# Joined pair operands, single-piece loads, VectorE copies and three product lumps in the backward pass of a fused attention and SwiGLU block

## The chip, the cores and the metric

The kernel runs on one core of a Trainium2 chip. The metric is the device time of one execution in microseconds (us), lower being better. Engines are named as in the profile: PE is TensorE, DVE is VectorE, ACT is ScalarE, POOL is GpSimd, SP is SyncE, which only issues DMAs here.

## The reference

The program computes a forward value and all gradients of a residual block in which attention and a SwiGLU feed-forward layer stand side by side on one layer norm. Sizes: 2048 tokens, model width 448, 16 heads of 28, feed-forward width 1792, bf16 inputs.

```python
xn  = layernorm(x)                                   # no scale, no bias
q, k, v = split_heads(xn @ wqkv)                     # 16 heads, Dh = 28
o   = softmax(q @ k.T * Dh**-0.5) @ v
out = x + merge_heads(o) @ wo + (silu(xn @ w_gate) * (xn @ w_up)) @ w_down
# outputs: out, and the gradients of <out, grad_out> for x, wqkv, wo, w_gate, w_up, w_down
```

## The kernel before, in words

The order of the instructions on each engine is written out by hand; nothing reorders them. The work has three stages.

**Stage one** (0 to about 642 us) is the layer norm, the projections, the attention forward and the feed-forward forward and backward. PE works through score products with feed-forward and weight-gradient products as fillers. At the end of the projections of a group of four heads (`proj_done`) POOL stores the transposed q, k and v of the group to DRAM tensors `qT_d`, `kT_d` and `vT_d`; at the end of each query block (`o_items`, its inner `do`) it stores the transposed, scaled output gradient to `dOT_d`. The attention's `load_pair` reads these back later.

**Stage two** (about 642 to 1465 us) is the attention backward. There are 8 pairs of heads (`pr`), two to a group (`g`). For each pair, four key chunks `kc` of 512 keys, and for each of them two windows of 8 query tiles: 512 *units* `k`, 64 *windows* `W`. The unit's place in its window is `pos`, 0 to 7. For a unit PE computes the scores of two heads into a PSUM tile (`sd`, line 851), and one unit later the gradients of the probabilities into another (`sd`, line 862). ACT takes the exponential (`E`, line 869). DVE multiplies the two into `ds` (line 880). Three units later `acc_mm` (line 748) adds the unit's share to the gradients of k and v. The pool `ps_sd` has three buffers: the scores of unit k need that `ds` of unit k-3 is done, and the second product of unit k needs that the exponential of unit k is done.

The gradient of q needs `ds` transposed, into a tile `dsT` per window. Six of the 8 units of a window are transposed by a DMA that SP issues right after `ds` is written (line 882). The two units in `TQ` are transposed on PE instead (`pe_transpose`, line 775, eight 128x128 transposes into the single PSUM buffer `aux`) and copied to `dsT` by `tr_out` (line 782): unit 1 of the window at the end of `pos` 6, by DVE, and unit 4 at `pos` 0 of the next window, by ACT. The pool of `ds` has 8 buffers: DVE can write `ds` of a unit only when the transposing DMA of the unit 8 earlier has landed. `dq_mm` (line 795) multiplies a window's `dsT` at `pos` 5 two windows later, and `dq_out` adds the result up on DVE at `pos` 6.

Each window also carries a *job* on PE from the list `jobs`, into the same `aux` buffer: a token tile of the block's output (`y`, 19 products of 448 columns, windows 1 to 16), a tile of one of two partial gradients of x (`dx`, 14 products), a chunk of the gradient of wqkv (`dwq`), or nothing. The products are issued in four lumps, at `pos` 1 to 4; ACT copies the result out at `pos` 4.

SP issues in one order: the job's tile for window W+2 at `pos` 0 (`job_load`, lines 660 to 666), the six transposes of a window, the transposes of finished gradients, and at `pos` 4 pieces of three lists: `pload`, the next pair's operands (`load_pair`, line 552); `gload`, the next group's (`load_group`, line 563); `wload`, the next weight matrix (line 539). A pair's operands are two tiles, `qT` and `kT`. Each has 64 partitions from one DRAM tensor and 64 from another, loaded in two column pieces: 8 DMAs of 128 KB. Up to two pieces of `pload`, one of `gload` and two of `wload` go out per window.

**The tail** (about 1465 us to the end) finishes the last chunks of the gradient of wqkv and, for each of 16 token tiles, adds up the gradient of x on PE and takes it back through the layer norm: `g_sb` on ACT, `junk`, `bb`, `cc` on DVE, `t1` on ACT (line 974), `t2` on DVE (976), the sum `dx` on POOL (979), the store by SP (980).

Of the kernel before, what the change touches and what calls it, by code (L numbers as in the profile page):

```python
# [10 lines left out]
ALU = mybir.AluOpType  # L11
AX = mybir.AxisListType
FP32 = mybir.dt.float32
BF16 = mybir.dt.bfloat16
# [3 lines left out]
S = 2048  # L18
D = 448
# [3 lines left out]
G = 4  # L23
HP = 32
P = 128
NT = S // P
# [11 lines left out]
def kernel(  # L38
# [19 lines left out]
    pe, act, dve, pool, sp = nc.tensor, nc.scalar, nc.vector, nc.gpsimd, nc.sync  # L58
# [4 lines left out]
    out1_d = out_1.rearrange("b (t p) d -> p (b t) d", p=P)  # L63

    dram = ctx.enter_context(tc.tile_pool(name="dram", bufs=1, space=DRAM))
    qT_d = dram.tile([G, P, S], BF16, name="qT_d")
    kT_d = dram.tile([G, P, S], BF16, name="kT_d")
    vT_d = dram.tile([G, P, S], BF16, name="vT_d")
    dOT_d = dram.tile([G, P, S], BF16, name="dOT_d")
    spq_d = dram.tile([G, P, NT * P], BF16, name="spq_d")  # L70
    spk_d = dram.tile([G, P, NT * P], BF16, name="spk_d")
    spo_d = dram.tile([G, P, NT * P], BF16, name="spo_d")
# [15 lines left out]
    xn_sp = const.tile([P, NT, DP], BF16, name="xn_sp")  # L88
# [109 lines left out]
    def proj_done(g):  # L198

        qT, kT, vT = (qk_tiles[(g, i)] for i in range(3))  # L200
        if g > 0:
            v = v_tiles[g] = qkp.tile([P, NT, P], BF16, name="v_sp")
            sp.dma_start_transpose(out=v[:], in_=vT[:])
        pool.dma_start(out=vT_d[g], in_=vT[:])
        pool.dma_start(out=qT_d[g], in_=qT[:])
        pool.dma_start(out=kT_d[g], in_=kT[:])

    def sp_layout(g, tq):
        s_ = stg.tile([P, NT, P], BF16, name="sp_stage")
# [256 lines left out]
    def o_items(g, qc, o_ps):  # L466
# [4 lines left out]
        st = {}  # L471
# [24 lines left out]
        def do(i):  # L496
            if i == 0:
                st["do"] = ps_f.tile([P, 4, P], FP32, name="f_ps")
            for c in range(4):
                pe.matmul(st["do"][:, i, :], lhsT=dyT[:, 4 * qc + i, c, :], rhs=woT[:, c, g * P:(g + 1) * P],  # L500
                          start=(c == 0), stop=(c == 3))
            if i < 3:
                return
            dps = st["do"][:].rearrange("p t (h r) -> p (t h) r", r=HP)
            rlb = st["rlc"][:].rearrange("p t h -> p (t h)")
            prod = op_.tile([P, 16, HP], FP32, name="prod")
            dve.tensor_tensor(out=prod[:], in0=dps,
                              in1=O_sp[g][:, tsl, :].rearrange("p t (h r) -> p (t h) r", r=HP), op=ALU.mult)
            delta = op_.tile([P, 16], FP32, name="delta")
            dve.tensor_reduce(out=delta[:], in_=prod[:, :, 0:DH], axis=AX.X, op=ALU.add)  # L510
            dOl = op_.tile([P, 4, P], BF16, name="dOl")
            dOv = dOl[:].rearrange("p t (h r) -> p (t h) r", r=HP)
            dve.tensor_tensor(out=dOv, in0=dps, in1=rlb.unsqueeze(2).to_broadcast([P, 16, HP]), op=ALU.mult)
            ndl = op_.tile([P, 16], FP32, name="ndl")
            dve.scalar_tensor_tensor(out=ndl[:], in0=delta[:], scalar=-1.0, in1=rlb, op0=ALU.mult, op1=ALU.mult)
            dve.tensor_copy(out=dOv[:, :, 28], in_=ndl[:])
            lo = op_.tile([P, 16], FP32, name="lo")
            dve.tensor_tensor(out=lo[:], in0=ndl[:], in1=dOv[:, :, 28], op=ALU.subtract)
            dve.tensor_copy(out=dOv[:, :, 29], in_=lo[:])
            pool.dma_start(out=spo_d[g, :, 4 * qc * P:(4 * qc + 4) * P], in_=dOl[:].rearrange("p t c -> p (t c)"))  # L520
            dT = op_.tile([P, 512], BF16, name="dOT")
            sp.dma_start_transpose(out=dT[:].rearrange("p (t s) -> p t s", t=4),
                                   in_=dOl[:].rearrange("p t c -> p (t c)"))
            pool.dma_start(out=dOT_d[g, :, qc * 512:(qc + 1) * 512], in_=dT[:])

        push([[(0.2, lambda i=i: tr(i)) for i in range(4)], [(0.26, lambda i=i: do(i)) for i in range(4)]]
             + (dwo_items(g) if qc == 3 else []), front=True, behind=1)
# [16 lines left out]

    def load_pair(pr, parts):

        g, r = pr // 2, 64 * (pr % 2)
        q = qkp.tile([P, S], BF16, name="qT")
        k = qkp.tile([P, S], BF16, name="kT")
        qd[pr] = (q, k)  # L550
        n = S // parts
        return [lambda i=i, dst=dst, r0=r0, src=src: sp.dma_start(
                    out=dst[r0:r0 + 64, i:i + n], in_=src[g, r:r + 64, i:i + n])
                for r0, srcs in ((0, (qT_d, kT_d)), (64, (dOT_d, vT_d)))
                for dst, src in zip((q, k), srcs) for i in range(0, S, n)]

    def load_group(g, parts, kpool):

# [206 lines left out]
                    in_=o[r:r + 64, :].rearrange("p (k s) -> p k s", k=2))  # L765
        sp_later.append(later)

    TQ = (1, 4)

    def pe_transpose(W, qi):  # L770

# [3 lines left out]
            pe.transpose(ps[:, i, :], ds[:, i // 4, (i % 4) * P:(i % 4 + 1) * P], ident_bf[:])  # L775
        st["tr"] = (ps, dsT[:, :, :, qi * P:(qi + 1) * P])

    def tr_out(eng):

        ps, dst = st["tr"]  # L780
        out, in_ = dst.rearrange("p j c q -> p (j c) q"), ps[:]
        act.copy(out=out, in_=in_) if eng is act else dve.tensor_copy(out=out, in_=in_)  # L782

    def dq_mm(W, half):
        pr, kc, w, _ = units[W * UW]
# [44 lines left out]
    for k in range(N + 2 * UW):  # L830
        W, pos = k // UW, k % UW
        if k < N:
# [7 lines left out]
            if pos == 4:  # L840
                if W == len(jobs) - 1:
                    wload.extend(load_w("wq", 2))
                for lst, n in ((pload, 2), (gload, 1), (wload, 2)):
                    for f in lst[:n]:
                        f()
                    del lst[:n]
# [3 lines left out]
            for j in range(2):  # L850
                pe.matmul(s_ps[:, j, :], lhsT=q[HP * j:HP * j + HP, qt * P:(qt + 1) * P],  # L851
                          rhs=kv[HP * j:HP * j + HP, kc * 512:(kc + 1) * 512],
                          start=True, stop=True, tile_position=(HP * j, 0))
        late_tr = pos == 0 and 1 <= W <= NW
        if 1 <= k <= N:
            pr, kc, w, qi = units[k - 1]
            q, kv = qd[pr]
# [10 lines left out]
            E[k] = ework.tile([P, 2, 512], BF16, name="E")  # L868
            act.activation(out=E[k][:], in_=s_ps[:], func=ACT.Exp, scale=SCALE)  # L869
        if late_tr:  # L870
            tr_out(act)
        job = jobs[W] if W < len(jobs) else None
        if pos == 6 and 2 <= W <= NW + 1:
            dq_out(W - 2)
# [9 lines left out]
        while sp_later:  # L884
            sp_later.pop(0)()

        if pos == 1:
            if 3 <= k < N + 3:
                acc_mm(k - 3)
            if job:  # L890
                st["aux"] = ps_x.tile([P, 512], FP32, name="aux")
                fillers = job_mms(W, st["aux"])
        if 1 <= pos < 5 and job:
            n = -(-len(fillers) // (5 - pos))
            for f in fillers[:n]:
                f()
            fillers = fillers[n:]
        if k == N + UW + 5:
            for c in range(4):
                if c % 2 == 0:  # L900
# [5 lines left out]
        if pos == 5 and 2 <= W <= NW + 1:  # L906
            dq_mm(W - 2, 0)
            dq_mm(W - 2, 1)
        if pos != 1 and 3 <= k < N + 3:
            acc_mm(k - 3)  # L910
        if pos == 4 and job:
            job_out(W, st["aux"])
        if pos == 6 and W < NW:
            pe_transpose(W, TQ[0])
            tr_out(dve)
    while sp_later:
        sp_later.pop(0)()
    ast.close()
# [2 lines left out]
    with ExitStack() as fin:  # L921
# [20 lines left out]
        for part in range(2):  # L942
            for c, (ps, m) in enumerate(last_dwq):
                for f in m[part][12 * (1 - part):]:
                    f()
                if part == 1:
                    dwq_out(3, c, ps)
        wq = wtile["wq"]
        for t in range(NT):
            if t % 2 == 0:  # L950
                load_c(t // 2 + 3, act)
# [5 lines left out]
            for n in range(3 * G):  # L957
# [14 lines left out]
                                     op0=ALU.mult, op1=ALU.mult)  # L972
            t1 = wk.tile([P, D], FP32, name="t1")
            act.activation(out=t1[:], in_=g_ps, func=ACT.Identity, scale=rstd[:, t:t + 1], bias=bb[:, 0:1])
            t2 = wk.tile([P, D], FP32, name="t2")
            dve.scalar_tensor_tensor(out=t2[:], in0=xn_sp[:, t, :D], scalar=cc[:, 0:1], in1=t1[:],
                                     op0=ALU.mult, op1=ALU.add)
            dx = wk.tile([P, D], BF16, name="dx")
            pool.tensor_tensor(out=dx[:], in0=t2[:], in1=dy_t[:, t, :], op=ALU.add)
            sp.dma_start(out=out1_d[:, t, :], in_=dx[:])  # L980
    cst.close()


# [28 lines left out]
```

## Time and profile before

| what | us |
|---|---|
| three runs | 1529.53, 1534.82, 1534.94 |
| median of them | 1534.82 |
| the profiled execution | 1534.68 |
| its span, first to last instruction | 1532.9 |
| mean granted clock of PE in it | 0.979 |

The times of the prediction below are worked out against the profiled execution, whose time is 0.14 us under the median of the runs. In the rows, "x57" is a count, "mean ns" is the mean duration of one instruction, and the last field tells for how long the engine stood idle before these instructions and what ended that. "SPq" is SP issuing a DMA. "issue" is time in which the engine waited for nothing that the profile shows.

### The profile page before, as it was taken

Reading aid. Unit: us, or ns where it says so; the run is one execution under the profiler, and the core shown is the slowest. Engines: PE = TensorE matmul, PEld = TensorE weight load, DVE = VectorE, ACT = ScalarE, POOL = GpSimd, SP = SyncE. Lnnn points to the kernel's source line nnn. Section 1 sums busy time; section 2 is a strip of 40 time slices with the busy share of each in tenths; the row PEclk is TensorE's granted clock in tenths of the full one; section 3 lists DMA queues with packets and bytes.
Section 4 is the critical chain, followed back from the end, with each engine's and each line's share of the span. In section 5 each row is a group of like instructions: output and inputs, shape, how many; then the busy total and the mean of one; then the engine's idle time right before and its main releaser. Section 6 shows DMA issues by size and latency. Waiting matters only on the chain.

```text
span 1532.9 us, 32019 instructions
## 1 busy us (share of the span) xinstructions
PE 1414.2 (92%) x12176; PEld 600.1 (39%) x12176; DVE 1100.7 (72%) x1421; ACT 1187.9 (77%) x1333; POOL 395.0 (26%) x664
## 2 busy tenths in 40 slices
PE   6899999999999999798989988989899899999987
PEld 3233333333333333333334344334345343544353
DVE  7664555656666667377878878888788788888925
ACT  6898998889888888576767777778778778788823
POOL 4332443344435444400111121101112101111033
PEclk9999999999999999889999999999999999999999
DMA  9976767878877799799999999999999999999984
GB/s 216 190 157 144 156 122 157 171 136 169 173 166 144 159 190 214 178 197 208 218 206 207 185 194 209 197 204 206 208 195 197 198 205 183 180 190 211 186 272 140
DMA packets 682106, 285.12 MB, mean 186 GB/s; under 512 B 637136, under 2 KB 650464, under 8 KB 681952
## 3 DMA queue, kind: packets, MB, share of 16 engines
q1 hardware_dynamic: 652016, 210.03, 75.5%
q0 software_dynamic: 25968, 64.53, 17.2%
q10 hardware_dynamic: 3968, 8.52, 1.7%
q8 instruction: 95, 1.56, 0.4%
q14 instruction: 59, 0.48, 0.1%
HBM read 67.34 MB, written 63.44 MB: 85 GB/s over the span
## 4 chain that ended last, share of the span: by engine, by line
PE 59%; ACT 13%; DMA 12%; DVE 8%; issue 6%; POOL 1%; SPq 0%; DVEq 0%; ACTq 0%; POOLq 0%
DMA dsT<-ds 9%; PE f_ps L356 8%; PE s_ps L599 7%; PE f_ps L382 7%; PE sd L851 6%; ACT E L869 5%; PE aux L718 5%; PE acc L748 4%; PE o_ps L581 4%; ACT eT L604 4%; PE aux L775 4%; DVE ds L880 4%; PE aux L795 3%; ACT dsT L782 3%; PE f_ps L180 3%
## 5 line engine op out<-in xcount | busy, mean ns | idle before, releaser
L880 DVE TENSOR_TENSOR ds<-sd,E 128x1024 bf16<-128x1024 f32 x512 | 611.5, 1219 | 134.0 <-PE sd L862 49.8
L869 ACT ACTIVATE E<-sd 128x1024 bf16<-128x1024 f32 x512 | 516.7, 1023 | 175.6 <-PE sd L862 136.5
L604 ACT ACTIVATE eT<-s_ps 128x1024 bf16<-128x1024 f32 x512 | 497.2, 1025 | 79.5 <-PE s_ps L599 76.1
L862 PE MATMUL sd<-kT,qT 32*128 32x512 bf16 x1024 | 203.4, 390 | 22.2 <-ACT E L869 21.3
L851 PE MATMUL sd<-kT,qT 32*128 32x512 bf16 x1024 | 202.7, 392 | 20.6 <-DVE ds L880 18.0
L748 PE MATMUL acc<-ds,v_sp 128*32 128x512 bf16 x1024 | 205.3, 396 | 0.7 <-DVE ds L880 0.7
L748 PE MATMUL acc<-E,O_sp 128*32 128x512 bf16 x1024 | 205.1, 396 | 0.2 <-ACT dkv_o L754 0.2
L599 PE MATMUL s_ps<-qT,kT 32*128 32x512 bf16 x1024 | 152.8, 383 | 10.1 <-ACT eT L604 7.9
L421 POOL DMA_DIRECT2D hd_d<-fT x168 | 126.9, 773 | 18.5 <-DVE fT L416 5.3
L382 PE MATMUL f_ps<-xnT,wgu 128*128 128x512 bf16 x448 | 117.6, 381 | 1.7 <-DVE w_sb L408 1.5
L763 POOL DMA_DIRECT2D dqkv_d<-dkv_o x64 | 39.2, 616 | 293.3 <-ACT dkv_o L754 291.4
L718 PE MATMUL aux<-W,ck 128*128 128x448 bf16 x448 | 107.5, 357 | 3.3
L851 PEld LDWEIGHTS <-qT 32*128 32x128 bf16 x1024 | 51.2, 91 | 150.0 <-issue 141.2
L581 PE MATMUL o_ps<-eT,v_sp 128*32 128x512 bf16 x1024 | 102.8, 391 | 0.0
L356 PE MATMUL f_ps<-xn_sp,f_sp 128*128 128x448 bf16 x448 | 99.7, 356 | 0.0
L599 PEld LDWEIGHTS <-kT 32*128 32x128 bf16 x1024 | 42.4, 90 | 143.5 <-issue 136.8
L748 PEld LDWEIGHTS <-O_sp 128*32 128x32 bf16 x1024 | 50.3, 93 | 113.5 <-issue 104.0
L775 PE MATMUL aux<-ident_bf,ds 128*128 128x128 bf16 x1024 | 81.3, 224 | 13.5 <-DVE dq_acc L807 6.5
L356 PEld LDWEIGHTS <-f_sp 128*128 128x128 bf16 x672 | 58.3, 98 | 78.6 <-issue 23.5
L862 PEld LDWEIGHTS <-qT 32*128 32x128 bf16 x1024 | 65.2, 91 | 60.5 <-issue 56.5
L775 PEld LDWEIGHTS <-ds 128*128 128x128 bf16 x1024 | 63.5, 99 | 42.4 <-issue 41.7
L394 DVE SCALAR_TENSOR_TENSOR g<-t_sb,f_ps 128x512 f32<-128x512 f32 x56 | 38.4, 686 | 54.0 <-ACT t_sb L392 53.9
(133 smaller groups left out, 1763.1 us busy)
## 6 DMA issues: line engine op xcount, KB each, us to landing
hd_d<-fT POOLq DMA_DIRECT2D x168, 128.0 KB, 4.6
ck<-hd_d SPq DMA_DIRECT2D x32, 448.0 KB, 4.3
ck<-hd_d SPq DMA_DIRECT2D x16, 576.0 KB, 4.9
dsT<-ds SPq DMA_TRANSPOSE x384, 4.2
dqkv_d<-dkv_o POOLq DMA_DIRECT2D x64, 64.0 KB, 3.8
dq_c<-dqkv_d ACTq DMA_DIRECT2D x5, 768.0 KB, 6.1
W<-wT_d SPq DMA_DIRECT2D x14, 224.0 KB, 3.6
out_dram<-dw_o POOLq DMA_DIRECT2D x28, 96.0 KB, 3.7
```

Of the source, the lines that this page charges most:

```text
L356: pe.matmul(acc[:, :D], lhsT=src[:, 12 * (t // 4) + 4 * wi + t % 4, :], rhs=rhs[:, t, :D], start=(t == 0), stop=(t == NT - 1))
L382: pe.matmul(st[name][:], lhsT=w(c), rhs=src[:, tsl, c, :], start=(c == 0), stop=(c == 3))
L581: pe.matmul(o_ps[HP * hh:HP * (hh + 1), :], lhsT=v[:, kt, HP * hh:HP * (hh + 1)], rhs=e[hh // 2][:, hh % 2, :], start=(kt == 0), stop=(kt ...
L599: pe.matmul(s_ps[:, j, :], lhsT=kT[r:r + HP, kt * P:(kt + 1) * P], rhs=qT[r:r + HP, qc * 512:(qc + 1) * 512], start=True, stop=True, tile_ ...
L604: act.activation(out=e[:], in_=s_ps[:], func=ACT.Exp, scale=SCALE)
L718: return [lambda n=n: pe.matmul(ps[:, :D], lhsT=t[:, n, :], rhs=w[:, n, :], start=(n == 0), stop=(n == NFC - 1)) for n in range(NFC)]
L748: pe.matmul(acc[r:r + HP, :], lhsT=src[:, qt, 64 * hp + HP * j:64 * hp + HP * j + HP], rhs=m[:, j, :], start=(qt == 0), stop=(qt == NT - 1 ...
L775: pe.transpose(ps[:, i, :], ds[:, i // 4, (i % 4) * P:(i % 4 + 1) * P], ident_bf[:])
L851: pe.matmul(s_ps[:, j, :], lhsT=q[HP * j:HP * j + HP, qt * P:(qt + 1) * P], rhs=kv[HP * j:HP * j + HP, kc * 512:(kc + 1) * 512], start=Tru ...
L862: pe.matmul(d_ps[:, j, :], lhsT=q[r:r + HP, qt * P:(qt + 1) * P], rhs=kv[r:r + HP, kc * 512:(kc + 1) * 512], start=True, stop=True, tile_p ...
L869: act.activation(out=E[k][:], in_=s_ps[:], func=ACT.Exp, scale=SCALE)
L880: dve.tensor_tensor(out=DS[k - 1][:], in0=d_ps[:], in1=E[k - 1][:], op=ALU.mult)
```

## The change

- **DRAM layout.** Four tensors become two with one entry per pair: `qdo_d` has q on the first 64 partitions and the output gradient on the others, `kv_d` has k and v. The stores in stage one are halved accordingly: `proj_done` issues 6 instead of 3, `do` 2 instead of 1, each with 64 partitions.
- **Loads.** `load_pair` makes a DMA of 128 partitions of each tile, in two column pieces: 4 DMAs of 256 KB for a pair. One piece goes out in an even window and one piece of `gload` in an odd one.
- **Transposes on PE.** `TQ` is (2, 6). Unit 2 is transposed at the end of `pos` 6 and copied after the multiplication of `pos` 7; unit 6 is transposed at `pos` 1 of the next window and copied before the multiplication there. DVE makes both copies.
- **Products.** A job's products go in three lumps, at `pos` 2 to 4; at `pos` 2 `acc_mm` stands ahead of the lump.
- **Tail.** `t2`, the sum and the store of a token tile are issued after `t1` of the next one (`finish`), and the last three sums are on DVE instead of POOL.

```diff
-    qT_d = dram.tile([G, P, S], BF16, name="qT_d")
-    kT_d = dram.tile([G, P, S], BF16, name="kT_d")
-    vT_d = dram.tile([G, P, S], BF16, name="vT_d")
-    dOT_d = dram.tile([G, P, S], BF16, name="dOT_d")
+    qdo_d = dram.tile([2 * G, P, S], BF16, name="qdo_d")
+    kv_d = dram.tile([2 * G, P, S], BF16, name="kv_d")
...
-        pool.dma_start(out=vT_d[g], in_=vT[:])
-        pool.dma_start(out=qT_d[g], in_=qT[:])
-        pool.dma_start(out=kT_d[g], in_=kT[:])
+        for hp in range(2):
+            rows = slice(64 * hp, 64 * hp + 64)
+            for dst, src in ((kv_d[2 * g + hp, 64:], vT), (qdo_d[2 * g + hp, :64], qT), (kv_d[2 * g + hp, :64], kT)):
+                pool.dma_start(out=dst, in_=src[rows, :])
...
-            pool.dma_start(out=dOT_d[g, :, qc * 512:(qc + 1) * 512], in_=dT[:])
+            for hp in range(2):
+                pool.dma_start(out=qdo_d[2 * g + hp, 64:, qc * 512:(qc + 1) * 512],
+                               in_=dT[64 * hp:64 * hp + 64, :])
...
-        return [lambda i=i, dst=dst, r0=r0, src=src: sp.dma_start(
-                    out=dst[r0:r0 + 64, i:i + n], in_=src[g, r:r + 64, i:i + n])
-                for r0, srcs in ((0, (qT_d, kT_d)), (64, (dOT_d, vT_d)))
-                for dst, src in zip((q, k), srcs) for i in range(0, S, n)]
+        return [lambda i=i, dst=dst, src=src: sp.dma_start(out=dst[:, i:i + n], in_=src[pr, :, i:i + n])
+                for i in range(0, S, n) for dst, src in ((q, qdo_d), (k, kv_d))]
...
-    TQ = (1, 4)
+    TQ = (2, 6)
...
-    def tr_out(eng):
-
+    def tr_out():
         ps, dst = st["tr"]
-        out, in_ = dst.rearrange("p j c q -> p (j c) q"), ps[:]
-        act.copy(out=out, in_=in_) if eng is act else dve.tensor_copy(out=out, in_=in_)
+        dve.tensor_copy(out=dst.rearrange("p j c q -> p (j c) q"), in_=ps[:])
...
-                for lst, n in ((pload, 2), (gload, 1), (wload, 2)):
+                for lst, n in ((pload, 1 - W % 2), (gload, W % 2), (wload, 2)):
...
-        late_tr = pos == 0 and 1 <= W <= NW
+        late_tr = pos == 1 and 1 <= W <= NW
...
         if late_tr:
-            tr_out(act)
+            tr_out()
...
-        if pos == 1:
-            if 3 <= k < N + 3:
-                acc_mm(k - 3)
-            if job:
-                st["aux"] = ps_x.tile([P, 512], FP32, name="aux")
-                fillers = job_mms(W, st["aux"])
-        if 1 <= pos < 5 and job:
+        if pos == 7 and W < NW:
+            tr_out()
+        acc = 3 <= k < N + 3
+        if pos == 2 and job:
+            st["aux"] = ps_x.tile([P, 512], FP32, name="aux")
+            fillers = job_mms(W, st["aux"])
+        lump = []
+        if 2 <= pos < 5 and job:
             n = -(-len(fillers) // (5 - pos))
-            for f in fillers[:n]:
-                f()
-            fillers = fillers[n:]
+            lump, fillers = fillers[:n], fillers[n:]
+        if acc and pos == 2:
+            acc_mm(k - 3)
+        for f in lump:
+            f()
+        if acc and pos != 2:
+            acc_mm(k - 3)
...
-        if pos != 1 and 3 <= k < N + 3:
-            acc_mm(k - 3)
...
         if pos == 6 and W < NW:
             pe_transpose(W, TQ[0])
-            tr_out(dve)
...
+        def finish(t, t1, cc):
+            t2 = wk.tile([P, D], FP32, name="t2")
+            dve.scalar_tensor_tensor(out=t2[:], in0=xn_sp[:, t, :D], scalar=cc[:, 0:1], in1=t1[:],
+                                     op0=ALU.mult, op1=ALU.add)
+            dx = wk.tile([P, D], BF16, name="dx")
+            add = pool if t < NT - 3 else dve
+            add.tensor_tensor(out=dx[:], in0=t2[:], in1=dy_t[:, t, :], op=ALU.add)
+            sp.dma_start(out=out1_d[:, t, :], in_=dx[:])
...
-            t2 = wk.tile([P, D], FP32, name="t2")
-            dve.scalar_tensor_tensor(out=t2[:], in0=xn_sp[:, t, :D], scalar=cc[:, 0:1], in1=t1[:],
-                                     op0=ALU.mult, op1=ALU.add)
-            dx = wk.tile([P, D], BF16, name="dx")
-            pool.tensor_tensor(out=dx[:], in0=t2[:], in1=dy_t[:, t, :], op=ALU.add)
-            sp.dma_start(out=out1_d[:, t, :], in_=dx[:])
+            if t > 0:
+                finish(t - 1, *held)
+            held = (t1, cc)
+        finish(NT - 1, *held)
```

1 line of the change is left out of this document (removed).

## The prediction

> **What bounds the kernel now.** I read the page first: the shares of the engines, the chain that ended last, and the groups of instructions, with shapes kept apart.
>
> ```profile
> PE 1414.2 (92%) x12176; PEld 600.1 (39%) x12176; DVE 1100.7 (72%) x1421; ACT 1187.9 (77%) x1333; POOL 395.0 (26%) x664
> DMA dsT<-ds 9%; PE f_ps L356 8%; PE s_ps L599 7%; PE f_ps L382 7%; PE sd L851 6%; ACT E L869 5%; PE aux L718 5%; PE acc L748 4%; PE o_ps L581 4%; ACT eT L604 4%; PE aux L775 4%; DVE ds L880 4%; PE aux L795 3%; ACT dsT L782 3%; PE f_ps L180 3%
> ...
> L880 DVE TENSOR_TENSOR ds<-sd,E 128x1024 bf16<-128x1024 f32 x512 | 611.5, 1219 | 134.0 <-PE sd L862 49.8 <-DMA dsT<-ds 46.6 <-issue 14.3
> L782 ACT COPY dsT<-aux 128x1024 bf16<-128x1024 bf16 x64 | 64.8, 1012 | 8.9 <-PE aux L775 1.5 <-DMA dsT<-ds 0.6
> L782 DVE COPY dsT<-aux 128x1024 bf16<-128x1024 bf16 x64 | 43.5, 680 | 0.6 <-DMA out_dram<-dwd_sb 0.6
> ```
>
> PE looks full on average, yet the longest single item of the chain is a DMA, the transpose of `ds`, and DVE stood still for 46.6 us until such a transpose had landed and freed a buffer of `ds`. That is stage two, where nearly the whole change lies. So next I asked how fast it advances: the multiplications of line 880 in three stretches (length, DVE busy, count, granted clock, DMA share).
>
> ```profile
> 657.20:858.20 201.00, 143.10 (x120) 0.98 1.10 209
> 858.20:1255.00 396.80, 296.18 (x250) 0.98 1.08 201
> 1255.00:1433.60 178.60, 143.61 (x121) 0.99 1.10 189
> ```
>
> A window has 8, and a count includes those cut by an edge: the stretches hold 15, 31 and 15 windows (1 to 15, 16 to 46, 47 to 61), at 201.0/15 = 13.4, 396.8/31 = 12.8 and 178.6/15 = 11.9 us a window. The last stretch is the undisturbed pace; the first two lose to something that comes and goes. The timelines of SP and of DVE in a slow window show it:
>
> ```profile
> 1101.17 1.22 SPq L552 DMA_DIRECT2D qT<-dOT_d  x2
> 1102.44 0.58 SPq L563 DMA_DIRECT2D vT<-spk_d  x1
> 1103.12 4.62 SPq L882 DMA_TRANSPOSE dsT<-ds  x3
> ...
> 1107.99 1.23 DVE L880 TENSOR_TENSOR ds<-sd,E 128x1024 bf16<-128x1024 f32 x1 [3.65 <-DMA dsT<-ds]
> ```
>
> Three loads stand in a row in SP's queue, the transposes come late behind them, and DVE then idles for 3.65 us for a buffer. The price list of SP:
>
> ```profile
> L552 SPq DMA_DIRECT2D qT<-qT_d x15: 470/587/1521, 558.4 to 1275.5; - x15
> L563 SPq DMA_DIRECT2D v_sp<-spq_d x7: 530/584/615, 579.3 to 1087.0; - x7
> L882 SPq DMA_TRANSPOSE dsT<-ds x381: 1231/1292/5342, 653.0 to 1454.6; - x191
> ```
>
> At the medians the six transposes of a window cost SP 6 x 1.29 = 7.8 us. The other work comes to about 2 us: half a transposed k/v gradient and a quarter of a transposed q gradient per window at the same price, and the job's tile. So SP has some 2 us to spare in 11.9 us, less where transposes run over the median, and a burst eats it.
>
> **The change, part by part.**
>
> *Loads.* Lines 552 and 563 are the comparison wanted: 128 KB on 64 partitions and 256 KB on 128 partitions both take SP 0.59 us (587 and 584 ns). So 56 issues become 28 in stage two and SP saves 28 x 0.587 = 16.4 us. More important, a window carries one such load where it had up to three: 0.6 us instead of 1.8, which fits into the spare time.
>
> What is lost to bursts: windows 1 to 46 last 201.0 + 396.8 = 597.8 us. The first 15 are `y` windows with five products more than a `dx` window, at 0.19 us each (a row below), so I estimate an undisturbed one at 11.8 + 0.9 = 12.7 us. 15 x 12.7 + 31 x 11.9 = 559 us; about 39 us is lost, a little less than DVE's 46.6 us of waits. I take three quarters of it back, **-30 us**: two loads of `W` a window remain, and the job's tiles. Ends: nothing, if the DMA engines (share 1.08 to 1.10) and not SP hold the transposes up, and -39.
>
> *Copies and places of the transposes.* A quiet window, DVE, ACT and PE (three timelines; `pos` 6 begins at 1357.60):
>
> ```profile
> 1357.56 0.68 DVE L810 SCALAR_TENSOR_TENSOR dq_acc<-aux,dq_acc 128x512 f32<-128x512 f32 x1
> 1358.16 1.21 DVE L880 TENSOR_TENSOR ds<-sd,E 128x1024 bf16<-128x1024 f32 x1
> 1359.29 0.68 DVE L782 COPY dsT<-aux 128x1024 bf16<-128x1024 bf16 x1
> 1359.89 2.34 DVE L880 TENSOR_TENSOR ds<-sd,E 128x1024 bf16<-128x1024 f32 x2
> ...
> 1361.32 1.01 ACT L782 COPY dsT<-aux 128x1024 bf16<-128x1024 bf16 x1
> ...
> 1357.60 0.39 PE L851 MATMUL sd<-kT,qT 32*128 32x512 bf16 x2
> ...
> 1359.10 0.39 PE L862 MATMUL sd<-kT,qT 32*128 32x512 bf16 x2
> ...
> 1360.34 0.39 PE L862 MATMUL sd<-kT,qT 32*128 32x512 bf16 x2 [0.20 <-ACT E L869]
> ...
> 1361.55 0.39 PE L851 MATMUL sd<-kT,qT 32*128 32x512 bf16 x2
> ```
>
> `pos` 6, 7 and 0 carry no lump. PE is quick there and is held by the exponential: `pos` 6's second product waits 1.50 us from 1357.60 for it, and `pos` 1 begins 3.95 us after `pos` 6. The remaining five places take 11.8 - 3.95 = 7.8 us on PE. In the changed order DVE has more to do in this light stretch. Starts in these rows are 0.60 us apart for a small operation and 1.13 to 1.17 for a multiplication, so from 1357.60 = 0: `dq_out` to 0.6, `ds` to 1.75, `ds` from 2.0 (half a us after its product) to 3.15, first copy to 3.75, `ds` to 4.9, second copy to 5.5, `ds` to 6.65. The scores of `pos` 2 need the `ds` that ends at 4.9, those of `pos` 3 the one at 6.65. Then PE's heavy places follow. A lump costs about 0.19 us a product plus 0.1 for the change of shape:
>
> ```profile
> 1351.85 0.93 PE L718 MATMUL aux<-W,ck 128*128 128x448 bf16 x4
> 1352.71 0.39 PE L748 MATMUL acc<-E,O_sp 128*32 128x512 bf16 x2
> ...
> 1353.37 0.74 PE L718 MATMUL aux<-W,ck 128*128 128x448 bf16 x3
> ...
> 1356.31 1.15 PE L795 MATMUL aux<-dsT,vT 128*32 128x512 bf16 x16
> ```
>
> A fourth product adds 0.93 - 0.74 = 0.19 us, and four take 1352.71 - 1351.85 = 0.86. The products of line 748 take about half of what lies between, 1353.37 - 1352.71 = 0.66 us, and those of the next unit's `sd` the other half: 0.66 us for a place without a lump. `dx` has lumps of 5, 5, 4: `pos` 3 takes 0.66 + 1.05 = 1.71, `pos` 4 1.52, and `pos` 5 with the 1.15 us of `dq_mm`, 0.1 of it under the next products, 1.72: 6.65 + 4.95 = 11.6 us. A single multiplication takes 1.22 rather than 1.15, and with that in the chain it is 11.9. Before it was 11.8. One lump fewer (-0.1) and ACT without its copy (64 x 1.012 us) are in this sum and buy little, since DVE now ends the light stretch. With `y`'s lumps of 7, 6, 6 the same chain gives 12.55 to 12.85 against 12.7. So the new order costs -0.2 to +0.25 us a window; I take +0.12, **+8 us** over 64 windows, ends -13 and +16. DVE's own work goes from 11.1 (8 x 1.219 + 2 x 0.68) to 11.8 us by isolated durations, 8 x 1.15 + 3 x 0.60 = 11.0 back to back.
>
> The places of the six DMA transposes change from runs of four and two to two runs of three. The first copy no longer waits for its transposes, since a multiplication stands ahead of it. The second stands ahead of a multiplication, and would delay it if DVE came there with nothing pending: the last rival.
>
> *Stage one.* POOL issues 12 more stores in `proj_done` and 16 more in `do`.
>
> ```profile
> L524 POOL DMA_DIRECT2D dOT_d<-dOT x16: 540/552/557, 85.7 to 646.7; - x16
> ```
>
> 28 x 0.55 = 15 us over 600 us of an engine that is 26% busy, hidden beside PE's fillers; uncovered, a store delayed by 0.55 us at the end would cost that. Zero, within 2 us.
>
> *Tail.*
>
> ```profile
> 1520.62 2.43 PE L958 MATMUL sd<-W,dq_c 128*128 128x448 bf16 x12
> ...
> 1525.75 0.69 DVE L976 SCALAR_TENSOR_TENSOR t<-xn_sp,cc,t 128x448 f32<-128x448 bf16 x1 [0.85 <-ACT t L974]
> ...
> 1528.48 0.69 DVE L976 SCALAR_TENSOR_TENSOR t<-xn_sp,cc,t 128x448 f32<-128x448 bf16 x1 [0.85 <-ACT t L974]
> ...
> L979 POOL TENSOR_TENSOR dx<-t,dy_t x16: 1029/1032/1076, 1489.0 to 1529.2; 128x448 bf16<-128x448 f32 x16
> ```
>
> DVE and ACT pass a tile back and forth every 1528.48 - 1525.75 = 2.73 us, and are late: PE ends at 1520.62 + 2.43 = 1523.05, and POOL's last sum at 1528.48 + 0.69 + 1.03 = 1530.2, 7.2 us later. With `t2` out of the loop PE's own 14 x 0.19 = 2.7 us or less a tile sets the pace; after PE's end there follow `g_sb`, `bb` and `t1`, and on DVE the previous tile's `t2` and sum and the last one's: some six operations of at most 0.7 us, 4.2 us. **-3 us**, ends 0 and -4.
>
> *Sum*: 1534.7 - 30 + 8 - 3 + 0 = 1509.7, so **1510 us**; the profiled execution stands for the median, which is 0.14 us above it.
>
> **The rivals.**
>
> *The whole burst loss goes and the order costs nothing* (17%): 1534.7 - 39 - 3 = 1493 us. For it: the last stretch, where DVE never waits for a transpose. Against it: the chain above.
>
> *The DMA engines, not SP's queue, make transposes late* (18%): the loads move the same bytes, nothing comes back, and 1534.7 + 8 - 3 = 1540 us remain. For it: a DMA share of 1.10 in the slow stretch. Against it: the last stretch has the same 1.10 with no such wait. The Trainium skill, page "DMA: Bandwidth & Descriptors", section Rules for kernel authors, holds that two transfers to disjoint partition halves run on the same engines anyway; by that rule the join removes issues alone and no data time, which is this rival's 1540 us if data time is what is late. The trace of before, with equal issue times for both sizes, doesn't contradict it.
>
> *DVE becomes the bound* (13%, slower): each moved copy lies on the path in full, at 64 x 0.680 = 43.5 us, while the burst gain stays: 1534.7 + 43.5 - 30 - 3 = 1545 us. It decides from the point where DVE reaches `pos` 1 without work pending, or where its 11.8 us exceed what PE leaves; the chain above leaves 0.4 us (transposes ready near 4.5, DVE free at 4.9). The Trainium skill, page "Perfetto Trace Analysis", section Optimizing Scalar/DVE Operations, speaks against the change here: where DVE is saturated, moving work to ScalarE may make sense. The trace agrees only in part: DVE's copy takes 0.680 us, ACT's 1.012.
>
> **How the numbers follow.** The forecast, between 1497 and 1525, has 52%; the rivals 17, 18 and 13. About 0.5% is what a measurement of this kernel can tell from no change: 1527 to 1542. Faster: the forecast, the first rival and a little of the second, 0.70; same 0.17, slower 0.13. The range holds the forecast, the first rival and the second: 1490 to 1541, and leaves out the last.
>
> **What would show it.** Right: DVE's idle time until `dsT<-ds` under 15 us (46.6 before); windows 1 to 46 near 12.2 us; PE's waits for `ds` at line 851 growing, as DVE ends the light stretch; line 552 with 28 issues of 0.6 us in stage two; the tail's period under 2.73 us. Wrong: that idle time stays near 40 us with single loads between transposes (the DMA engines), or the undisturbed last stretch goes over 12.3 us a window (DVE).

## The result, and the profile after

| | before | after |
|---|---|---|
| median of four runs, us | 1533.2 (1529.53 to 1534.94) | 1516.62 (1516.1 to 1518.34) |
| ratio, 95% interval | | 0.9897 (0.9875 to 0.9919) |
| the profiled execution, us | 1534.68 | 1516.44 |
| its span, us, and granted clock | 1532.9, 0.979 | 1514.3, 0.985 |

The change makes the kernel 16.6 us faster by the medians, 18.2 us by the two profiled executions; the forecast was 24.7 us against the profiled one. The page of the changed kernel, the lines that answer to those shown of before: PE's and DVE's busy time, the chain that ended last by line, the multiplication, and the copies of the units that PE transposed.

```profile
PE 1395.4 (92%) x12176; PEld 581.7 (38%) x12176; DVE 1128.3 (75%) x1488; ACT 1129.7 (75%) x1269; POOL 409.5 (27%) x689
...
PE f_ps L355 7%; PE sd L847 7%; DMA dsT<-ds 7%; PE s_ps L597 7%; PE f_ps L381 6%; PE acc L746 6%; DVE ds L876 5%; PE aux L716 5%; ACT E L865 4%; ACT eT L602 4%; PE o_ps L579 4%; PE aux L773 4%; PE aux L710 4%; PE sd L858 3%; PE f_ps L178 3%
...
L876 DVE TENSOR_TENSOR ds<-sd,E 128x1024 bf16<-128x1024 f32 x512 | 611.8, 1219 | 83.5 <-DMA dsT<-ds 36.4
...
L778 DVE COPY dsT<-aux 128x1024 bf16<-128x1024 bf16 x128 | 87.2, 681 | 0.0
```

DVE's idle time ahead of `ds` fell from 134.0 to 83.5 us. The part that a transposing DMA ended fell only from 46.6 to 36.4, less than two profiles of one and the same stage two differ (46.6 and 58.4, below), and that DMA still has 7% of the chain (9% before). DVE took over 64 copies (87.2 us instead of 43.5), with no idle time ahead of them. The same three stretches of stage two as before, windows 1 to 15, 16 to 46 and 47 to 61 (length, DVE busy in line 876, count, granted clock, DMA share, GB/s):

```profile
658.10:860.58 202.48, 143.79 (x120) 0.97 1.11 209
860.58:1243.77 383.19, 295.83 (x248) 0.99 1.10 207
1243.77:1419.61 175.84, 143.55 (x120) 0.99 1.09 195
```

That is 13.50, 12.36 and 11.72 us a window, against 13.4, 12.8 and 11.9: the middle stretch gave 13.6 us, the last 2.8; the first took 1.5, which is within the scatter of such a figure (5 us, below). The same light stretch as in the prediction, from the timelines of DVE and of PE (`pos` 6 begins at 1356.42):

```profile
1350.35 4.80 DVE L876 TENSOR_TENSOR ds<-sd,E 128x1024 bf16<-128x1024 f32 x4
...
1356.57 0.68 DVE L809 SCALAR_TENSOR_TENSOR dq_o<-aux,dq_acc 128x512 bf16<-128x512 f32 x1
1357.16 2.48 DVE L876 TENSOR_TENSOR ds<-sd,E 128x1024 bf16<-128x1024 f32 x2
1359.56 0.68 DVE L778 COPY dsT<-aux 128x1024 bf16<-128x1024 bf16 x1
1360.16 1.22 DVE L876 TENSOR_TENSOR ds<-sd,E 128x1024 bf16<-128x1024 f32 x1
1361.29 0.68 DVE L778 COPY dsT<-aux 128x1024 bf16<-128x1024 bf16 x1
1361.89 1.22 DVE L876 TENSOR_TENSOR ds<-sd,E 128x1024 bf16<-128x1024 f32 x1
```

```profile
1356.42 0.39 PE L847 MATMUL sd<-kT,qT 32*128 32x512 bf16 x2
...
1360.00 0.39 PE L847 MATMUL sd<-kT,qT 32*128 32x512 bf16 x2
...
1361.50 0.39 PE L847 MATMUL sd<-kT,qT 32*128 32x512 bf16 x2
```

DVE works through six operations without a pause, as the prediction's chain had it, and PE reaches `pos` 1 after 1360.00 - 1356.42 = 3.58 us where it took 3.95. From the first `ds` of this window (1350.35) to that of the next (1361.89) there are 11.54 us. A slow window, by SP's timeline:

```profile
962.47 6.04 SPq L878 DMA_TRANSPOSE dsT<-ds  x3
968.61 1.72 SPq L759 DMA_TRANSPOSE dkv_sp<-dkv_o  x1
970.42 0.53 SPq L552 DMA_DIRECT2D qT<-qdo_d  x1
971.04 4.26 SPq L878 DMA_TRANSPOSE dsT<-ds  x3
```

A single load of 0.53 us now stands between the transposes, as intended. But three transposes take SP 6.04 us, 2.0 each, where the median is 1.3: SP is occupied by transposes that are slow themselves. Summed over the 384 records, a transpose takes SP 1.554 us on average (1.527 before) at a median of 1.296. What lies over the median, 384 x 0.258 = 99 us, is six times what the halved loads took off SP's queue (16 us).

### The profile page after: what moved, and what is told of

Read it like the earlier page. It is cut to its first block, busy times and chain, and to the rows that moved or that the text cites. A ratio compares the mean times of both kernels' runs of the same rounds, so it can differ in the third digit from the quotient of the medians.

```text
span 1514.3 us, 31832 instructions
## 1 busy us (share of the span) xinstructions
PE 1395.4 (92%) x12176; PEld 581.7 (38%) x12176; DVE 1128.3 (75%) x1488; ACT 1129.7 (75%) x1269; POOL 409.5 (27%) x689
## 3 DMA queue, kind: packets, MB, share of 16 engines
q0 software_dynamic: 26416, 64.53, 18.2%
## 4 chain that ended last, share of the span: by engine, by line
PE 65%; DMA 10%; DVE 10%; ACT 9%; issue 4%; SPq 0%; DVEq 0%; POOL 0%; ACTq 0%; POOLq 0%
PE f_ps L355 7%; PE sd L847 7%; DMA dsT<-ds 7%; PE s_ps L597 7%; PE f_ps L381 6%; PE acc L746 6%; DVE ds L876 5%; PE aux L716 5%; ACT E L865 4%; ACT eT L602 4%; PE o_ps L579 4%; PE aux L773 4%; PE aux L710 4%; PE sd L858 3%; PE f_ps L178 3%
## 5 line engine op out<-in xcount | busy, mean ns | idle before, releaser
L876 DVE TENSOR_TENSOR ds<-sd,E 128x1024 bf16<-128x1024 f32 x512 | 611.8, 1219 | 83.5 <-DMA dsT<-ds 36.4
L716 PE MATMUL aux<-W,ck 128*128 128x448 bf16 x448 | 101.4, 355 | 0.0
L778 DVE COPY dsT<-aux 128x1024 bf16<-128x1024 bf16 x128 | 87.2, 681 | 0.0
```

Of the source, the lines that this page charges most:

```text
L716: return [lambda n=n: pe.matmul(ps[:, :D], lhsT=t[:, n, :], rhs=w[:, n, :], start=(n == 0), stop=(n == NFC - 1)) for n in range(NFC)]
L876: dve.tensor_tensor(out=DS[k - 1][:], in0=d_ps[:], in1=E[k - 1][:], op=ALU.mult)
```

## The experiments

Mean window in us by stretch, from one profiled execution each; the last column is DVE's wait for a transposing DMA. The tail-only kernel has the stage two of before and the loads-with-tail kernel has that of the loads-only one, so these pairs show the scatter of such a figure: 0.3 a window in the first stretch, 0.1 in the second, 0.1 in the last. The same pairs give the scatter of the wait: 46.6 against 58.4 us, and 52.0 against 47.1. Only larger differences are read, so a wait of 36.4 us is not shown to be less than one of 46.6.

| kernel | median us | ratio (95%) | W 1-15 | W 16-46 | W 47-61 | wait |
|---|---|---|---|---|---|---|
| before | 1533.2 | | 13.40 | 12.80 | 11.91 | 46.6 |
| after | 1516.62 | 0.9897 (0.9875 to 0.9919) | 13.50 | 12.36 | 11.72 | 36.4 |
| loads only | 1521.04 | 0.9928 (0.9903 to 0.9953) | 13.18 | 12.53 | 11.98 | 52.0 |
| order only | 1532.06 | 0.9996 (0.9974 to 1.0018) | 13.67 | 12.67 | 11.62 | 45.6 |
| tail only | 1530.38 | 0.9988 (0.9974 to 1.0003) | 13.73 | 12.78 | 11.89 | 58.4 |
| loads with tail | 1520.73 | 0.9899 (0.987 to 0.9927) | 13.27 | 12.65 | 11.89 | 47.1 |
| one copy moved to DVE | 1531.01 | 1.0000 (0.9983 to 1.0017) | 13.72 | 12.68 | 11.82 | 37.2 |
| after, job tiles by POOL | 1549.83 | 1.0144 (1.0074 to 1.0213) | 14.34 | 12.63 | 12.48 | 75.5 |
| after, job tiles cut | 1488.54 | 0.9720 (0.9687 to 0.9754) | 12.52 | 11.96 | 11.66 | 15.4 |
| after, 12 buffers of ds | 1516.28 | 0.9907 (0.9876 to 0.9939) | 12.54 | 12.42 | 11.89 | 11.8 |
| after, late copy by ACT | 1511.75 | 0.9861 (0.9829 to 0.9893) | 13.15 | 12.31 | 11.96 | 29.0 |
| same, 10 buffers | 1514.83 | 0.9871 (0.9829 to 0.9913) | 13.07 | 12.52 | 11.90 | 23.6 |
| same, 8 + 4 buffers | 1517.02 | 0.9902 (0.9867 to 0.9936) | 13.07 | 12.55 | 11.90 | 12.0 |
| same, third unit on PE | 1609.8 | 1.0495 (1.0468 to 1.0522) | 14.49 | 13.70 | 13.64 | 0.0 |

Each ratio stands against runs of the kernel before on the same chip: their median was 1531.89 us for the loads, the order, the tail and the moved copy by themselves, 1535.32 for loads with tail, 1532.92 for the four kernels that start from the changed one, and 1533.84 for the last three.

**The parts one by one.** *Loads only*, the kernel before with the joined tensors and one piece a window:

```diff
+    qdo_d = dram.tile([2 * G, P, S], BF16, name="qdo_d")
+    kv_d = dram.tile([2 * G, P, S], BF16, name="kv_d")
...
+        return [lambda i=i, dst=dst, src=src: sp.dma_start(out=dst[:, i:i + n], in_=src[pr, :, i:i + n])
...
+                for lst, n in ((pload, 1 - W % 2), (gload, W % 2), (wload, 2)):
```

> The kernel before with the joined tensors and the loads one piece at a time, and nothing else of the change. If bursts in SP's queue were the loss (the prediction's step), 20 to 30 us less than before and DVE's wait for dsT under 20 us. If the DMA engines make the transposes late, within 4 us of before and that wait still 35 to 50 us.

It gave 0.72%, 11 us (7 to 15). Its waits on DVE, and then those of the kernel before:

```profile
DVE ds L878 <- DMA dsT<-ds: 52.0, 42, 5.0
DVE ds L878 <- PE sd L860: 43.1, 109, 1.1
DVE ds L878 <- issue: 14.2, 35, 0.6
...
DVE ds L878 <- ACT E L867: 2.7, 2, 1.6
```

```profile
DVE ds L880 <- PE sd L862: 49.8, 119, 2.1
DVE ds L880 <- DMA dsT<-ds: 46.6, 33, 3.6
DVE ds L880 <- issue: 14.3, 34, 0.6
DVE ds L880 <- ACT E L869: 12.6, 11, 2.2
```

Neither expectation came. The wait for transposes, on which the prediction had built the term, did not fall. What fell are the waits put down to `E` and to `sd`, 16.6 us together; but the pairs with the same stage two differ in each of these by about 4 us too (`sd` 49.8 and 47.6, 43.1 and 47.1; `E` 12.6 and 8.2, 2.7 and 5.4). The loads' gain is real, but it is not shown to be the one that was argued, and what the 11 us are stays open.

*Order only*, the kernel before with the new places, DVE's copies and the three lumps:

```diff
-    TQ = (1, 4)
+    TQ = (2, 6)
...
-            tr_out(act)
+            tr_out()
...
-        if 1 <= pos < 5 and job:
+        if 2 <= pos < 5 and job:
```

> The kernel before with TQ (2, 6), both copies on DVE and three lumps; its loads and tail are those of before. By the prediction's sum 8 us more than before. If the changed kernel's quiet windows of 11.54 us (11.78 before) come from this part, 64 x 0.24 = 15 us less, whatever the loads do.

Neither: -0.6 us, with an interval from -4.0 to +2.8. The last stretch, where DVE hardly waits for transposes, came down from 11.91 to 11.62 us a window, more than the scatter; the time did not follow. (The profiled execution took 1526.76 us, 5.3 less than the median of the ten runs.)

*Tail only*, `finish` after the next tile's `t1`:

```diff
+            if t > 0:
+                finish(t - 1, *held)
+            held = (t1, cc)
```

> The kernel before with the tail's tiles in two steps and the last three sums on DVE. Both theories: 3 to 4 us less (1531 from 1534.7), from the period of 2.73 us and the wait after PE's end; stage two as before.

-1.8 us, with an interval from -4.0 to +0.5. In its profile the time from the last `ds` to the end went from 76.3 to 70.0 us, in the changed kernel's to 72.6; the loads-only kernel, whose tail is the old one, has 73.2, so one profile does not settle 3 us here.

*Loads with tail*, the change without its order, tests whether the order counts once the loads come singly:

> The kernel before with two of the change's three parts: the operands joined and loaded a piece at a time, and the tail's tiles in two steps; the order, the copies and the lumps of stage two stay as before. What it is short of the full change (ratio 0.9897) is what the order is worth beside the other two. If the order is worth nothing (it measured 1.000 alone), the ratio is 0.989 to 0.991, as the full change. If the parts only add up, loads 0.9928 times tail 0.9988 give 0.9916, and the order has given 0.2% (3 us). If the shorter quiet windows of the order (11.6 us against 11.9) count only once the loads come one at a time, the ratio is 0.993 to 0.996 and the order gives 5 to 8 us beside the others.

0.9899 against 0.9897: the full gain, without the order. Beside the other two parts it is worth nothing that these runs can tell (the two intervals allow 5 us either way).

**Is DVE the bound?** *One copy moved to DVE*, alone, in its old place ahead of a multiplication:

```diff
-            tr_out(act)
+            tr_out(dve)
```

> The kernel before with one word changed: DVE instead of ACT copies the late transposed unit, in its old place at pos 0. If the moved copy lies on the path in full: 64 x 0.68 = 43 us more. If DVE has room and only the order counts: 0 to 15 us more, quiet windows 11.8 to 12.0 us. If ACT's copy was what held pos 0 and 1: less than before.

1.0000, within 0.0017: the moved copy does not lie on the path in full, and the rival that priced it so, at 43.5 us, falls. The reverse, the changed kernel with the *late copy by ACT*:

```diff
-            tr_out()
+            tr_out(act)
```

> The changed kernel with ACT copying the second transposed unit (pos 1), as ACT did in the kernel before, but at the new place. If DVE's chain through the light places sets the undisturbed window (11.54 us): 11.2 to 11.5 us there and 3 to 12 us less. If ACT's copy delays the exponential of the next unit as much as DVE gains: no change.

By the medians it is 5 us faster than the changed kernel and has the lowest time of all kernels that do the whole work, 1511.75 us; its interval lies wholly under the kernel before, but meets that of the changed kernel, so those 5 us are not settled. They did not come as expected either: the undisturbed windows grew instead of shrinking (11.96 us in the last stretch against 11.72). DVE's chain alone thus does not set them; ACT's copy costs more there than DVE gains by losing its own.

**SP's queue or the DMA engines?** *Job tiles by POOL* takes them and their `x` from SP's queue:

```diff
-            sp.dma_start(out=t[:], in_=hd_d[j[1], :, :G + NFC, :])
+            pool.dma_start(out=t[:], in_=hd_d[j[1], :, :G + NFC, :])
...
-            sp.dma_start(out=x[:], in_=x_d[:, j[1], :])
+            pool.dma_start(out=x[:], in_=x_d[:, j[1], :])
...
-            sp.dma_start(out=t[:, :NFC], in_=hd_d[j[2], :, G + NFC * (1 + j[1]):G + NFC * (2 + j[1]), :])
+            pool.dma_start(out=t[:, :NFC], in_=hd_d[j[2], :, G + NFC * (1 + j[1]):G + NFC * (2 + j[1]), :])
```

> The changed kernel with the job's tiles (and x's tile) issued by POOL instead of SP: the same bytes, 64 issues fewer in SP's queue (about 39 us of its 731). If SP's queue is what is still late, DVE's wait for dsT falls from 36 to under 15 us and the time by 15 to 25 us, to about 1495. If the DMA engines are late, within 5 us of the changed kernel.

33 us slower than the changed kernel, which neither expectation had. SP issued 490 DMAs in stage two instead of 552, and was busy for 769 us instead of 731. The DMA issues (count, KB each, median us from issue to landing), first of the changed kernel, then of this one, and the transposes' SP times (min/median/max ns) and landing times (min/median/max us) of this one:

```profile
ck<-hd_d SPq DMA_DIRECT2D x32, 448.0 KB, 4.2
...
dsT<-ds SPq DMA_TRANSPOSE x384, 4.2
```

```profile
ck<-hd_d POOLq DMA_DIRECT2D x32, 448.0 KB, 5.4
...
dsT<-ds SPq DMA_TRANSPOSE x384, 4.5
```

```profile
L878 SPq DMA_TRANSPOSE dsT<-ds x384: 1231/1297/7998, 651.2 to 1474.4; - x192
...
DMA to landing us min/median/max: 3.0/4.5/14.7
```

The tiles land later, and so do the transposes beside them, one of them after 14.7 us (8.6 at most in the changed kernel). The Trainium skill, page "DMA: Bandwidth & Descriptors", section Rules for kernel authors, holds that spreading DMAs over issuing engines gives no bandwidth and saves only the sequencer's issue time. The run agrees on the first (198, 203 and 182 GB/s in the three stretches, 209, 207 and 195 in the changed kernel); the issue time that was saved came back with interest, since SP's mean per transpose rose from 1.554 to 1.729 us.

The run changes more than the queue, though. The tiles' 26 MB went over from `q1 hardware_dynamic` to `q0 software_dynamic`, and POOL issues them at other moments: the first three with their rows of `x` within 3 us (649.70 to 652.41), where SP had issued two of them before the first transpose (645.40 and 646.49) and the third at 662.67. Six transposes then held SP for 15 us:

```profile
657.77 14.96 SPq L878 DMA_TRANSPOSE dsT<-ds  x6
```

So it shows that a shorter SP queue does not help; how the 33 us divide between queue, moments and load is not shown.

*Job tiles cut* leaves the issues in their places and takes the bytes away (`n` is one 128x128 block from the fourth tile on; the `dx` tiles likewise):

```diff
-            t = ckp.tile([P, NFC + G, P], BF16, name="ck")
-            sp.dma_start(out=t[:], in_=hd_d[j[1], :, :G + NFC, :])
+            t, n = ck_tile(G + NFC)
+            sp.dma_start(out=t[:, :n], in_=hd_d[j[1], :, :n, :])
```

> The changed kernel with the job's tiles kept in three fixed buffers: from the fourth job on a load keeps its issue in SP's queue but brings one 128x128 block instead of 14 or 18, so most products use old operands. About 20 MB of 110 MB in stage two are left out. If the DMA engines are late: DVE's wait for dsT under 10 us, windows 1 to 15 near 12.6 us, 20 to 30 us less. If SP's queue is late: within 8 us of the changed kernel.

28 us faster than the changed kernel, from the same number of issues. The same three stretches:

```profile
658.64:846.49 187.85, 143.89 (x120) 1.00 1.05 186
846.49:1217.27 370.78, 296.33 (x248) 1.00 1.05 187
1217.27:1392.12 174.85, 143.62 (x121) 0.99 1.03 173
```

14.6 and 12.4 us come from the first two stretches and 1.0 from the last. DVE's wait falls to 15.4 us, and SP's mean per transpose to 1.453 us. So the bytes that the DMA engines move, and not the number of issues, made both late. The last stretch had a share of 1.09 without losing much, so the share alone doesn't tell late from not late. Part of the 27 us may be PE's clock: in windows 1 to 46 the changed kernel has five slots of 3.4 us at a granted clock of 0.50 (the first from 672.3 to 675.7, after a pause of PE of 2.0 us), this one a single slot. Four slots at half speed are at most 7 us by estimate; whether they only follow from the waits was not tested.

**Can the wait be bridged?** *12 buffers of ds* let DVE run further ahead of the transposes:

```diff
-    dsw = ast.enter_context(tc.tile_pool(name="dsw", bufs=8))
+    dsw = ast.enter_context(tc.tile_pool(name="dsw", bufs=12))
```

> The changed kernel with 12 instead of 8 buffers for ds. If transposes are late only for moments (bursts) and the average rate is enough: the wait for dsT under 10 us and 10 to 25 us less. If the rate itself is the limit in windows 1 to 46, the wait only comes later and the time stays within 5 us.

The wait fell to 11.8 us and the time stayed. Its waits on DVE:

```profile
DVE ds L876 <- PE sd L858: 49.5, 90, 5.1
DVE ds L876 <- DMA dsT<-ds: 11.8, 9, 3.8
DVE ds L876 <- DMA out_dram<-dwd_sb: 9.5, 1, 9.5
```

The first stretch, with all its bytes in place (length, DVE busy, count, granted clock, DMA share, GB/s), went as fast as with the tiles cut:

```profile
671.21:859.29 188.08, 143.97 (x120) 1.00 1.09 211
```

So in this profile the average rate was enough for the 15 `y` windows at this load, and a longer ring bridged the lateness there (twelve buffers in two pools, below, took 13.07 us a window). In the later stretches it gained nothing: two windows of the middle one took 17.2 and 17.8 us. Stage two got 7.6 us shorter (788.0 after 795.6) but began 12.8 us later: the first `ds` waited for a store of stage one, `dwd_sb`, 9.5 us. I take it that the larger pool lies over that tile. So I put the four extra buffers into a pool behind the others (with ACT's late copy), and beside it tried ten buffers in one pool:

```diff
+    dsw2 = ast.enter_context(tc.tile_pool(name="dsw2", bufs=4))
...
-            DS[k - 1] = dsw.tile([P, 2, 512], BF16, name="ds")
+            DS[k - 1] = (dsw if (k - 1) % 12 < 8 else dsw2).tile([P, 2, 512], BF16, name="ds")
```

> The changed kernel with ACT copying the second transposed unit (as the last run, 1511.75 us) and four more ds buffers, in a pool of their own behind the others, so that the first of them is written ten microseconds into stage two. If the twelve buffers took the wait for the transposes away (36.4 to 11.8 us) and only the late start of stage two gave it back (12.8 us), that start is as before (first ds near 645 us), the wait stays near 12 us and the time is 1511.75 less some 5 to 8 us: 1504 to 1507 us. If the wait is only moved (ds comes earlier, transposes land as late, the next user is PE with dsT), stage two stays at 790 to 793 us and the time at 1510 to 1513 us.

> As the run beside it, but ten ds buffers in the one pool (the ring two units longer). If a longer ring is what is missing, half of the wait is gone and the time is 1507 to 1511 us, less by what the first ds waits at the start of stage two; if the larger pool again lies over memory that stage one still uses, the first ds comes up to 13 us later (near 658 us) and the time is 1512 to 1518 us.

Neither came as expected. The first `ds` came nearly on time (649.1 and 646.4 us), the wait was 12.0 and 23.6 us (29.0 with eight buffers), and neither kernel is faster than the eight buffers at 1511.75 us. With twelve the time went elsewhere, by the waits of DVE and of PE:

```profile
DVE ds L878 <- PE sd L860: 101.2, 183, 8.5
DVE ds L878 <- DMA dsT<-ds: 12.0, 9, 3.0
```

```profile
PE aux L680 <- DMA dq_sp<-dq_o: 7.8, 1, 7.8
PE aux L717 <- DMA W<-wT_d: 3.4, 1, 3.4
```

DVE now waits for PE, and PE waited once 7.8 us for a finished gradient's transpose, which SP had issued behind six others (11.1 us) and three loads, and once 3.4 us for a weight. Two windows took 21.6 and 17.7 us. The transposes are as late as before (4.43 us to landing on average, 4.35 with eight buffers); their lateness merely reaches another user.

*A third unit on PE* takes transposes away without leaving anything out:

```diff
-    TQ = (2, 6)
+    TQ = (2, 6, 4)
...
+        mid_tr = pos == 0 and 1 <= W <= NW
+        if mid_tr:
+            pe_transpose(W - 1, TQ[2])
...
+        if mid_tr:
+            tr_out(act)
```

> The changed kernel with ACT copies for the late units, and a third unit of each window transposed by PE (copied by ACT), so five of eight go through DMA instead of six; nothing is left out. If the DMA engines' load is the rest of the limit (as the smaller tiles showed with 20 MB left out), the wait for the transposes falls from 36 to under 20 us and their landing from 4.37 to under 4.2 us; what PE pays is 64 times eight transposes (near 0.6 us), 38 us, of which the time keeps what PE's idle time cannot take: from 1500 us (all hidden) to 1545 us (all paid). If PE has become the bound in windows without waits (it is 92% busy), the time comes out slower, 1530 to 1545 us, although the wait falls.

The wait is gone, and the kernel is 98 us slower than with two. Its transposes on SP, and what PE waited for in stage two:

```profile
L884 SPq DMA_TRANSPOSE dsT<-ds x320: 1231/1233/3428, 657.7 to 1534.1; - x160
```

```profile
PE aux L773 <- DVE dsT L779: 32.5, 59, 0.6
PE aux L773 <- ACT dsT L779: 24.8, 56, 0.4
PE sd L859 <- ACT E L869: 23.9, 60, 0.8
```

With five transposes a window even the median issue is at the minimum, 1.233 us, and the mean landing is 3.95 us: DMA is relieved. But each window has grown by 98/64 = 1.5 us, not the 0.6 that eight transposes take on PE. 57 us are waits for the single `aux` buffer, in which three transposed units, a job and `dq` now follow each other; I had left that out of the expectation. PE's busy time in stage two grew by 52 us besides (727.1 to 779.2), more than the 38 us expected for the transposes, at a granted clock of 0.94 there instead of 0.98. How the 98 us divide is not shown.

## Why the prediction was right or wrong

- **What bounds it.** That stage two's first 46 windows lose time to late transposes was right: relieving the DMA engines brought 27 us back there, of which up to 7 may be the clock. That they come late because loads stand ahead of them in SP's queue is what no run bore out: with the loads halved and spaced DVE's wait for them was 52.0 us, with 64 more issues taken from the queue 75.5 us.
- **The loads, -30 us: this term was mis-sized.** Alone they gave 11 us (7 to 15). The step that failed is taking three quarters of the 39 us back because one load of 0.6 us "fits into the spare time" of SP. That spare time was worked out with the median transpose of 1.29 us; the mean is 1.53, so six take 9.2 us and not 7.8, and most of the 2 us is gone. The very row that the prediction read as a late start has three transposes in 4.62 us, 1.54 each. The second rival, the DMA engines, was right for the part that stayed, at least for the 20 MB that were cut. Its own time (1540 us) was wrong, since it allowed the loads nothing. By the rule quoted there from the Trainium skill, page "DMA: Bandwidth & Descriptors", section Rules for kernel authors, the join is worth its issues alone; the 11 us contain both the join and the spacing of the loads and do not tell these apart.
- **The order, +8 us, ends -13 and +16.** Measured alone: -0.6 us (-4.0 to +2.8). The chain by hand came out nearly right in size: DVE works through the light stretch without a pause, and the quiet window of 11.54 us is at its lower end of 11.6. I took the middle between 11.6 and 11.9, of which the latter came from the isolated 1.22 us of a multiplication; in the rows above, `ds` starts at 1360.16 and the copy behind it at 1361.29, 1.13 us later, as the rows of before had it. The Trainium skill, page "Perfetto Trace Analysis", section Optimizing Scalar/DVE Operations, states that a profiled latency contains a write acknowledgement which overlaps with the next instruction; these 0.09 us agree in kind. That freeing ACT of its copy would "buy little" was wrong for quiet windows: with that copy back on ACT they take 11.8 to 12.0 us again, as before. At -0.2 us a window the whole of stage two would have gained 13 us. It did not, which fits windows in which a DMA sets the pace, so that being ready earlier buys nothing: of windows 1 to 46 of the changed kernel, 21 are over 0.3 us longer than the same windows with the job tiles cut. That last step is argued from the runs, not shown by one.
- **DVE as the bound, 1545 us.** Refuted at that price by the moved copy at 1.0000.
- **Stage one, 0.** The first `ds` comes at 646.1 us instead of 644.8, inside the 2 us allowed.
- **The tail, -3 us.** Rows of the changed kernel's tail:

```profile
1498.19 0.68 DVE L950 SCALAR_TENSOR_TENSOR t<-xn_sp,cc,t 128x448 f32<-128x448 bf16 x1
...
1500.84 0.68 DVE L950 SCALAR_TENSOR_TENSOR t<-xn_sp,cc,t 128x448 f32<-128x448 bf16 x1
...
1510.75 0.62 DVE L954 TENSOR_TENSOR dx<-t,dy_t 128x448 bf16<-128x448 f32 x1
```

```profile
1504.84 2.43 PE L966 MATMUL sd<-W,dq_c 128*128 128x448 bf16 x12
```

  The period is 2.65 us (2.73 before), as the prediction had it, and 1510.75 + 0.62 - 1504.84 - 2.43 = 4.1 us follow PE's end, where the prediction counted 4.2 and before had 7.2. The tail by itself measured -1.8 us (-4.0 to +0.5), which allows the -3 and does not show it.
- **The signs it named.** Line 552 has 28 issues of 0.57 us in stage two, and the tail's period fell: as said. Idle time under 15 us (it was 36.4) and 12.2 us a window (12.7 over windows 1 to 46) did not come. PE's waits for `ds` hardly grew: at the scores they fell from 18.0 to 9.8 us, but 8.9 us of waits for `ds` came up at the second product (line 858), 18.7 together. "Idle stays near 40 us with single loads between transposes" was named as the sign of the DMA engines, and that is what the trace showed.
- **The sum.** 1510 against 1516.6: 19 us of gain too much for the loads, 8 us of cost too much for the order, and a tail within its interval. These corrections alone would give 1521; the other 4 us lie within the parts' intervals and the start, which was 1.5 us over the median. Two errors of opposite sign made the number better than its working, so its closeness is luck; the range of 1490 to 1541 would have held the right sum too.

## What to carry to other kernels

A queue's spare time is worked out from the mean issue and not from the median: where the mean lies far over the median (here 1.53 over 1.29 us), the issues themselves are being held up, and thinning the queue may bring little (here 11 of the 39 us). A way to tell a full queue from loaded DMA engines is to keep the issues and cut the bytes, and then to keep the bytes and move the issues; here the first gave 28 us and the second cost 33, though moving the issues also moved them in time. A wait that an extra buffer takes away is only a gain if the next user of the late data has slack: two kernels with twelve buffers brought DVE's wait to 12 us from 36.4 and 29.0, and neither was shown to be faster for it.

## What the runs showed of the hardware

- The time for which SP is held by a transpose varies with what else the DMA engines move, 1.23 us at the least and 8.0 at the most; its mean was 1.354 us with five a window, 1.453 with the job tiles cut, 1.554 in the changed kernel, and 1.729 with the tiles issued by POOL.
- The same 448 KB load took 4.2 us to land from SP's queue and 5.4 us from POOL's, where it was also issued at other moments, and the transposes on SP's queue landed later (4.37 to 4.93 us on average).
- One profiled execution's stretch of 15 windows differs by up to 5 us between kernels whose stage two is the same, though the medians of their times agree to 0.2%, and DVE's wait for a transposing DMA by up to 12 us; a stretch or a wait is evidence only over that.
